# Delta-rule attention with two MoE layers: fewer warm-up products, shorter norms, and the first word fetch behind the solve's matrices

## The chip, the cores and the metric

One core of a Trainium2 chip runs the whole program in one launch. The metric is device time in microseconds. The kernel before takes 926.25 us (median of 3 runs, 925.52 to 926.77).

## The reference

Attention by the delta rule: for each of 4 x 8 heads a 48 x 48 state is updated over 768 steps, with normalised keys; then two MoE layers over all 3072 tokens.

```python
k_n = k / (np.linalg.norm(k, axis=-1, keepdims=True) + 1e-06)
for t in range(S):
    kt, vt, bt = (k_n[:, :, t], v[:, :, t], beta[:, :, t, None])
    y[:, :, t] = np.einsum('bhd,bhde->bhe', q[:, :, t], state)
    v_old = np.einsum('bhde,bhd->bhe', state, kt)
    state = state + bt[:, :, :, None] * np.einsum('bhd,bhe->bhde', kt, vt - v_old)
# x: attention output, 3072 x 384
h = np.maximum(x @ w_in, 0.0)                                # 384 x 2048
x = h * h @ w_out                                            # 2048 x 384
h = np.maximum(np.maximum(x @ w1, x @ w2), x @ w3)           # 384 x 768 each
return h @ w_out2                                            # 768 x 384
```

## The kernel before

The 768 steps are cut into 12 chunks of 64. Within a chunk the recurrence becomes a triangular system for each head. Its matrix is the Gram matrix of the chunk's keys, scaled by beta and by the squared norms. Each 64 x 64 system is solved as two halves of 32, one matrix on each of 128 partitions for two chunks at a time: that is the tile `M`, a view of `buf`, and `solve` on VectorE. The halves are merged with products on TensorE (`pZ`, `pW`), then come `pU` (the solved values), `pY` (the outputs), `pT` (a transpose) and `pD` (the state). After chunk 0 the MoE of chunk c runs on TensorE while the attention of chunk c + 1 is woven in between. The second MoE layer runs when all chunks are done.

All weights arrive as the 64-bit words of the arrays, two 32-bit halves to a value. ScalarE brings sign and exponent into place (`signed`: a Prelu at L103 and a Copy at L108), VectorE joins the halves (L120), ScalarE casts to the high part (L124), VectorE subtracts to get the low part (L128). A block of `w_in` is 384 KB; 12 blocks have tiles of their own (`rawp`), the others take turns (`raw`, `big`, `buf`). In this text "words" are these fetches, and a block's "signing" is L103 and L108.

The head, up to the first MoE product, runs in this order:

- Warm-up: NWARM products on TensorE (L716) on a zeroed tile, while the keys of chunks 0 and 1 are loaded (L772): first the keys of four half chunks, then their queries, alternately on the queues of SyncE (SP) and ScalarE.
- Gram products (`grams`, L784), four with keys alone, four with the queries. The first four are copied to SBUF by ScalarE and VectorE (L789) and stored to HBM as `kk` (L185). The second four are masked on VectorE (L798); two of them are stored by POOL (L800).
- `start32` (L292) loads beta (L299) and M: two DMAs per chunk, L302, from `kk` in HBM. Here chunk 0 is loaded by POOL, chunk 1 by SP.
- `prep` copies the diagonal (L247), then `norms` and `weighted` (L217 to L231) compute the norm `nm`, the row scale `r` = -beta/nm^2 and `a` = beta/nm^2. POOL clears the upper part of M with an affine select (L236), VectorE scales M by `r` (L237) and sets the diagonal (L238).
- `solve`: 30 pairs of a product and a sum (L283, L285) and a last scaling (L286).
- The result goes to HBM as `xt`, half by SP and half by ScalarE (L323), and `load_x` brings it back in another layout (`xb`, L342, `x1`, L350), half on each of the two queues for chunk 0.
- Meanwhile SP issues the words (L93) and the keys of chunks 2 and 3 (L833). ScalarE signs the first 12 blocks and copies the Gram matrices of chunks 2 and 3 (L841), POOL masks them (L846, eight operations).

Each engine carries out its instructions in one fixed order. For the greater part a scheduler sets that order when the program is built, from an estimate of its own of every instruction's time. `behind(a, b)` puts a after b on an engine without a wait. A DMA is issued by its engine in that order too and waits there for what it needs; it then runs beside the engine. DMAs from SP and ScalarE take one of eight semaphores in turn, and each waits until the earlier DMA with the same semaphore has landed.

Of the kernel before, what the change touches and what calls it, by code (L numbers as in the profile page):

```python
# [13 lines left out]
ALU = mybir.AluOpType  # L14
# [13 lines left out]
NF = FF // 128  # L28
# [11 lines left out]
def delta_moe(ctx, tc, kc, ab, kt, vt, beta, beta32, beta16, kq, w_in, w_out, w1, w2, w3, w_out2, out):  # L40
    nc = tc.nc
    vec, act, pool = nc.vector, nc.scalar, nc.gpsimd
# [31 lines left out]
    after, abs_after, cast_after, raw_after, x_after, raws = [], [], [], [], [], []  # L74
    parted, last_gl, last_gh = [], [None], [None]
    loose, casts = set(), []
    NR, NP = 4, 12
# [11 lines left out]
    def fetch(src, shape, dma):  # L89
        raw = raw_tile(shape)  # L90
        names = "k n" if len(shape) == 2 else "n"
        flat = "k (n t)" if len(shape) == 2 else "(n t)"
        raws.append(dma.dma_start(raw.rearrange(f"p {names} t -> p {flat}"), src).ins)  # L93
        for i in raw_after + x_loaded[-1:] * (NF < len(raws) <= 2 * NF):
            behind(raws[-1], i)
        return raw

# [52 lines left out]
    kcts, kss = [], []  # L150
# [32 lines left out]
    def kk_store(c, p, kk, dma=nc.sync):  # L183
        for t in range(2):
            dma.dma_start(kk_d[c][:, t, U2 * p:U2 * p + U2], kk[64 * t:64 * t + 64])  # L185
# [25 lines left out]
    def norms(ss, n, u, pool_):  # L211

        s0 = pool_.tile([128, n], F32, name="s0", tag="s0", bufs=1)
        r = pool_.tile([128, n], F32, name="r", tag="r", bufs=1)
        nm = pool_.tile([128, n], F32, name="nm", tag="nm", bufs=1)
        s0, r, nm = s0[0:u], r[0:u], nm[0:u]
        act.activation(out=s0, in_=ss, func=AF.Sqrt)  # L217
        vec.tensor_scalar(out=s0, in0=s0, scalar1=1e-19, scalar2=None, op0=ALU.max)
        vec.reciprocal(r, s0)
        vec.tensor_mul(out=r, in0=r, in1=ss)  # L220
        vec.tensor_add(out=r, in0=r, in1=s0)
        vec.tensor_scalar(out=nm, in0=r, scalar1=0.5, scalar2=1e-6, op0=ALU.mult, op1=ALU.add)
        return nm, r, s0

    def weighted(ss, n, u, bt, a, pool_):

        nm, r, s0 = norms(ss, n, u, pool_)
        vec.reciprocal(r, nm)
        vec.tensor_mul(out=s0, in0=r, in1=r)
        vec.tensor_mul(out=a, in0=s0, in1=bt)  # L230
        vec.tensor_scalar(out=r, in0=a, scalar1=-1.0, scalar2=None, op0=ALU.mult)  # L231
        return nm, r

    def strict(M, n, u, r, eng):

        selected[0] = pool.affine_select(out=M, in_=M, pattern=[[-1, n], [1, n]], compare_op=ALU.is_ge, fill=0.0, base=0, channel_multiplier=0).ins  # L236
        eng.tensor_mul(out=M, in0=M, in1=r.unsqueeze(1).broadcast_to([u, n, n]))  # L237
        eng.memset(diagonal(M, n), 1.0)  # L238

    selected, loaded, prep_after = [None], [None], []  # L240

    def diagonal(M, n):
        return M.rearrange("p j i -> p (j i)")[:, 0:n * n:n + 1]

    def prep(M, n, u, bt, a, pool_, eng=vec):
        ss = pool_.tile([128, n], F32, name="ss", tag="ss", bufs=1)[0:u]
        i = vec.tensor_copy(ss, diagonal(M, n))  # L247
        for j in prep_after:
            behind(i.ins, j)
        nm, r = weighted(ss, n, u, bt, a, pool_)  # L250
        strict(M, n, u, r, eng)
        return nm

    pinned, seen = {}, [None]
# [14 lines left out]
    def behind(ins, before):  # L269

        tc.add_manual_dep(ins, before.name, mybir.DependencyInfo(mybir.DependencyClass.NoSync, mybir.DependencyReason.DATA), reason="order")
# [108 lines left out]
    ops, normed, solved, solve_after, x_loaded = [], [], [], [], []  # L380
# [324 lines left out]
    if True:  # L705
        pro = ExitStack()
        pkp = pro.enter_context(tc.tile_pool(name="pkp", bufs=1))

        NWARM = 8
        ks_more = pkp.tile([128, 2, U2, C], F32, name="ks_more", tag="ks_more")  # L710
        warm = ks_more[:, 0, 0:2].rearrange("p u s -> p (u s)")
        vec.memset(warm, 0.0)
# [12 lines left out]
        def solve32(g, load=(nc.sync, nc.sync), store=((nc.sync,) * 2,) * 2, landing=0):  # L725
            M, a, ready, norm = start32(g, load)
            for _ in range(landing):
                yield
            if landing:
                prep_after[:] = last_gl  # L730
            nm = ready()
            if not g:
                normed.append(norm(nm))
            yield
            for n, i in enumerate(solve(vec, M, 32, 64 * len(HALVED[g]), a, tmp32)):
                for j in solve_after:
                    behind(i.ins, j)
                ops.append(i.ins)
                if g and n == (24 if g == 1 else 8):
                    norm(nm)  # L740
                yield
            finish32(g, M, store)
# [44 lines left out]
        for n, (c, p) in enumerate(todo):  # L787
            pg = grams(n, 0, (p1, at)[n % 2])
            kk_ends[p] = (vec.tensor_copy if p else act.copy)(kss[n][:, 0], pg).ins  # L789
            kk_store(c, p, kss[n][:, 0], (nc.sync, act)[p])  # L790
        p_stores = []
        for n, (c, p) in enumerate(todo):
            pg = grams(n, 1, (p1, at)[n % 2])
# [4 lines left out]
            prep_after[:] = [vec.tensor_mul(out=ks, in0=pg, in1=mask.unsqueeze(1).broadcast_to([128, U2, C])).ins]  # L798
            if c:
                p_stores.append(pool.dma_start(p_d[c][:, U2 * p:U2 * p + U2], ks).ins)  # L800
        first_solve = solve32(0, (pool, nc.sync), ((nc.sync, act), None))
        next(first_solve)
        prep_after.clear()
        raw_after[:] = loaded
# [241 lines left out]
```

## Time and profile before

| what | us |
|---|---|
| median of 3 runs | 926.25 |
| the profiled execution | 926.38 |
| its span, first to last instruction | 924.4 |
| TensorE busy, share of the span | 868.5, 94% |
| VectorE (DVE) busy | 475.8, 51% |
| ScalarE (ACT) busy | 376.0, 41% |
| GpSimd (POOL) busy | 146.6, 16% |

The rows come from the profiled execution; times are from the start of its span. A busy TensorE is not one at its peak: its matmuls are pipelined and their ends are modelled. The granted clock (PEclk) is a share of full speed, 1.00 or 0.50 at a moment, a mean in a stretch. A DMA's time to landing is counted from its issue. The DMA share is the mean busy share of 16 engines and can be above 1 where the packets of several queues overlap.

### The profile page before, as it was taken

The numbers are of one execution on the slowest core, as the hardware profiler recorded it, in microseconds if no ns is written. First come the engines' busy times: TensorE is split into PE (matmuls) and PEld (weight loads), VectorE is DVE, ScalarE is ACT, GpSimd is POOL, SyncE is SP. The second block draws the span as 40 slices with busy tenths as digits, with TensorE's granted clock in tenths as the row PEclk, the third lists the DMA queues.
The fourth block names the chain that finished last, engine by engine and source line by source line (L and its number), as shares of the span: only waits on it lengthen the run. The fifth ranks groups of instructions, "written<-read, shape, count | busy, mean of one in ns | idle before, by whom it ended". The sixth has DMA issues, their size and how long they took to land.

```text
span 924.4 us, 26481 instructions
## 1 busy us (share of the span) xinstructions
PE 868.5 (94%) x11422; PEld 843.0 (91%) x11422; DVE 475.8 (51%) x1068; ACT 376.0 (41%) x799; POOL 146.6 (16%) x241
## 2 busy tenths in 40 slices
PE   5439899899999999999999999999999999999998
PEld 5328888799999999999999999999999999999998
DVE  2978886288348734873586364457232322323221
ACT  1447853353445344544453556564121221212111
POOL 2323121411331133122313300002000000000000
PEclk8557999899999999999999999999999999999999
DMA  9987634732852284337434551334110101000000
GB/s 196 309 256 226 202 83 133 194 96 67 207 160 66 85 215 133 78 87 190 104 82 104 143 146 53 102 107 136 38 37 31 35 18 43 10 26 9 18 18 35
DMA packets 122596, 98.82 MB, mean 107 GB/s; under 512 B 77440, under 2 KB 102832, under 8 KB 122480
## 3 DMA queue, kind: packets, MB, share of 16 engines
q1 hardware_dynamic: 101824, 58.42, 24.1%
q0 software_dynamic: 11584, 32.22, 12.2%
q10 hardware_dynamic: 9072, 6.49, 2.4%
q8 instruction: 90, 1.47, 0.7%
q14 instruction: 26, 0.21, 0.1%
HBM read 72.45 MB, written 24.64 MB: 105 GB/s over the span
## 4 chain that ended last, share of the span: by engine, by line
PE 84%; DVE 8%; DMA 3%; ACT 2%; issue 1%; ACTq 0%; SPq 0%; DVEq 0%
PE p L954 24%; PE px L592 21%; PE p L572 20%; PE po L971 8%; PE pY L514 2%; PE pU L464 2%; DVE buf L283 2%; DVE buf L285 2%; PE pk L180 1%; PE pW L420 1%; DMA kct<-in_kc_dram 1%; PE pZ L411 1%; PE pA L445 1%; DMA raw<-in_moe_w_out_dram 1%; DVE gl L581 1%
## 5 line engine op out<-in xcount | busy, mean ns | idle before, releaser
L954 PE MATMUL p<-x_h,w 128*128 128x384 f32 x864 | 220.1, 336 | 0.0
L592 PE MATMUL px<-wout,gh 128*128 128x384 f32 x768 | 200.6, 342 | 0.4 <-ACT gh L580 0.4
L572 PE MATMUL p<-xh,win_h 128*128 128x256 f32 x576 | 169.6, 294 | 2.0 <-DVE gl L581 1.4
L572 PE MATMUL p<-xl,win_h 128*128 128x256 f32 x576 | 164.0, 285 | 0.3 <-DVE xl L536 0.3
L572 PE MATMUL p<-xh,win_l 128*128 128x256 f32 x576 | 164.0, 285 | 0.0
L954 PEld LDWEIGHTS p<-x_h,w 128*128 128x128 f32 x864 | 156.2, 188 | 0.0
L954 PE MATMUL p<-x_l,w 128*128 128x384 f32 x432 | 145.2, 336 | 0.0
L581 DVE TENSOR_TENSOR gl<-p,gh 128x512 fp32r<-128x512 f32 x96 | 66.2, 690 | 144.8 <-ACT gh L580 144.5
L592 PEld LDWEIGHTS px<-wout,gh 128*128 128x128 f32 x768 | 135.6, 190 | 1.9 <-ACT gh L580 0.6
L592 PE MATMUL px<-wout,gl 128*128 128x384 f32 x384 | 129.6, 337 | 0.0
L578 ACT ACTIVATE p<-p 128x512 f32<-128x512 f32 x96 | 55.9, 582 | 176.0 <-PE p L572 176.0
L572 PEld LDWEIGHTS p<-xh,win_h 128*128 128x128 f32 x576 | 111.0, 193 | 5.3 <-DVE gl L581 1.9
L572 PEld LDWEIGHTS p<-xl,win_h 128*128 128x128 f32 x576 | 111.1, 193 | 0.6 <-DVE xl L536 0.5
L572 PEld LDWEIGHTS p<-xh,win_l 128*128 128x128 f32 x576 | 111.4, 193 | 0.0
L960 DVE TENSOR_TENSOR mx<-p,mx 128x384 f32<-128x384 f32 x48 | 26.7, 557 | 126.7 <-PE p L954 126.6
L954 PEld LDWEIGHTS p<-x_l,w 128*128 128x128 f32 x432 | 81.2, 188 | 0.0
L962 ACT CAST hh<-mx 128x384 fp32r<-128x384 f32 x48 | 24.6, 513 | 125.8 <-DVE mx L961 125.8
L592 PEld LDWEIGHTS px<-wout,gl 128*128 128x128 f32 x384 | 72.7, 189 | 0.0
L285 DVE TENSOR_TENSOR buf<-buf 128x30 f32<-128x30 f32 (+9 forms) x180 | 61.1, 339 | 6.1
L283 DVE TENSOR_TENSOR buf<-buf 128x30 f32<-128x30 f32 (+9 forms) x180 | 60.6, 337 | 5.0
L580 ACT CAST gh<-p 128x512 fp32r<-128x512 f32 x96 | 56.4, 587 | 2.6
L579 ACT ACTIVATE p<-p 128x512 f32<-128x512 f32 x96 | 55.9, 583 | 2.6
(166 smaller groups left out, 1290.7 us busy)
## 6 DMA issues: line engine op xcount, KB each, us to landing
kq<-in_kc_dram POOLq DMA_DIRECT2D x22, 448.0 KB, 5.3
raw<-in_moe_w_dram SPq DMA_DIRECT2D x18, 384.0 KB, 3.5
raw<-in_moe_w_out_dram SPq DMA_DIRECT2D x16, 384.0 KB, 4.4
p<-p POOLq DMA_DIRECT2D x22, 256.0 KB, 3.6
rawp<-in_moe_w_in_dram SPq DMA_DIRECT2D x12, 384.0 KB, 10.3
v<-in_vt_dram POOLq DMA_DIRECT2D x24, 192.0 KB, 3.0
ktp<-in_kt_dram POOLq DMA_DIRECT2D x24, 192.0 KB, 3.6
x<-xs SPq DMA_DIRECT2D x48, 96.0 KB, 3.2
```

The lines of the kernel that those rows point to most:

```text
L283: eng.tensor_tensor(out=tv, in0=M[:, 0:j, j].unsqueeze(2).broadcast_to([u, j, m]), in1=M[:, j, j + 1:n].unsqueeze(1).broadcast_to([u, j, m ...
L285: yield eng.tensor_tensor(out=M[:, 0:j, j + 1:n], in0=M[:, 0:j, j + 1:n], in1=tv, op=ALU.add)
L572: pe.matmul(p1[:, j], w[:, k, f], x[c][:, k], start=n == 0 and j == 0, stop=n == 8, skip_group_check=True)
L578: act.activation(out=p1, in_=p1, func=AF.Relu)
L579: act.activation(out=p1, in_=p1, func=AF.Square)
L580: last_gh[0] = act.copy(gh, p1).ins
L581: last_gl[0] = vec.tensor_sub(out=gl, in0=p1, in1=gh.bitcast(F32)).ins
L592: g = pe.matmul(px[:, h, 0:DM], x[:, j, hs], w, start=f == 0 and i == 0, stop=f == NF - 1 and i == 2, skip_group_check=True)
L954: pe.matmul(p, w[i][:, k, fs], x[:, k], start=n == 0, stop=n == 8)
L960: vec.tensor_max(out=t, in0=ps[1], in1=t)
L962: act.copy(hh[:, f], t2)
L971: pe.matmul(po[:, 0:DM], x[:, f, js], w[:, f], start=i == 0, stop=i == 17)
```

## The change

It has five parts. The warm-up has 4 products instead of 8. The norm drops its factor 0.5 until later: `nm` is first twice the norm, and `r` is formed with -4 to make up for it. After M is scaled, two operations bring `nm` to its value and make `a` from `r`. The first word fetch gets a memset of one column of its tile, on POOL, ordered behind the affine select; the fetch waits for the memset, and the next eleven are ordered behind the first. Of the Gram stores three pairs go to SP and one to ScalarE, instead of two and two. M and beta of chunk 0 are loaded by SP and of chunk 1 by ScalarE.

```diff
--- before.py
+++ after.py
@@ -90,8 +90,10 @@
         raw = raw_tile(shape)
         names = "k n" if len(shape) == 2 else "n"
         flat = "k (n t)" if len(shape) == 2 else "(n t)"
+        if not raws:
+            behind(pool.memset(raw[:, 0, 0, 0:1], 0).ins, selected[0])
         raws.append(dma.dma_start(raw.rearrange(f"p {names} t -> p {flat}"), src).ins)
-        for i in raw_after + x_loaded[-1:] * (NF < len(raws) <= 2 * NF):
+        for i in raws[:1] * (1 < len(raws) <= NP) + raw_after + x_loaded[-1:] * (NF < len(raws) <= 2 * NF):
             behind(raws[-1], i)
         return raw
 
@@ -218,24 +220,23 @@
         vec.tensor_scalar(out=s0, in0=s0, scalar1=1e-19, scalar2=None, op0=ALU.max)
         vec.reciprocal(r, s0)
         vec.tensor_mul(out=r, in0=r, in1=ss)
-        vec.tensor_add(out=r, in0=r, in1=s0)
-        vec.tensor_scalar(out=nm, in0=r, scalar1=0.5, scalar2=1e-6, op0=ALU.mult, op1=ALU.add)
+        vec.scalar_tensor_tensor(out=nm, in0=r, scalar=2e-6, in1=s0, op0=ALU.add, op1=ALU.add)
         return nm, r, s0
 
     def weighted(ss, n, u, bt, a, pool_):
 
         nm, r, s0 = norms(ss, n, u, pool_)
-        vec.reciprocal(r, nm)
-        vec.tensor_mul(out=s0, in0=r, in1=r)
-        vec.tensor_mul(out=a, in0=s0, in1=bt)
-        vec.tensor_scalar(out=r, in0=a, scalar1=-1.0, scalar2=None, op0=ALU.mult)
+        vec.tensor_mul(out=s0, in0=nm, in1=nm)
+        vec.reciprocal(a, s0)
+        vec.scalar_tensor_tensor(out=r, in0=bt, scalar=-4.0, in1=a, op0=ALU.mult, op1=ALU.mult)
         return nm, r
 
     def strict(M, n, u, r, eng):
 
         selected[0] = pool.affine_select(out=M, in_=M, pattern=[[-1, n], [1, n]], compare_op=ALU.is_ge, fill=0.0, base=0, channel_multiplier=0).ins
-        eng.tensor_mul(out=M, in0=M, in1=r.unsqueeze(1).broadcast_to([u, n, n]))
+        scaled = eng.tensor_mul(out=M, in0=M, in1=r.unsqueeze(1).broadcast_to([u, n, n])).ins
         eng.memset(diagonal(M, n), 1.0)
+        return scaled
 
     selected, loaded, prep_after = [None], [None], []
 
@@ -248,7 +249,9 @@
         for j in prep_after:
             behind(i.ins, j)
         nm, r = weighted(ss, n, u, bt, a, pool_)
-        strict(M, n, u, r, eng)
+        scaled = strict(M, n, u, r, eng)
+        for t, x, by in ((nm, nm, 0.5), (a, r, -1.0)):
+            behind(vec.tensor_scalar(out=t, in0=x, scalar1=by, scalar2=None, op0=ALU.mult).ins, scaled)
         return nm
 
     pinned, seen = {}, [None]
@@ -706,7 +709,7 @@
         pro = ExitStack()
         pkp = pro.enter_context(tc.tile_pool(name="pkp", bufs=1))
 
-        NWARM = 8
+        NWARM = 4
         ks_more = pkp.tile([128, 2, U2, C], F32, name="ks_more", tag="ks_more")
         warm = ks_more[:, 0, 0:2].rearrange("p u s -> p (u s)")
         vec.memset(warm, 0.0)
@@ -787,7 +790,7 @@
         for n, (c, p) in enumerate(todo):
             pg = grams(n, 0, (p1, at)[n % 2])
             kk_ends[p] = (vec.tensor_copy if p else act.copy)(kss[n][:, 0], pg).ins
-            kk_store(c, p, kss[n][:, 0], (nc.sync, act)[p])
+            kk_store(c, p, kss[n][:, 0], (nc.sync, act)[n == 3])
         p_stores = []
         for n, (c, p) in enumerate(todo):
             pg = grams(n, 1, (p1, at)[n % 2])
@@ -798,7 +801,7 @@
             prep_after[:] = [vec.tensor_mul(out=ks, in0=pg, in1=mask.unsqueeze(1).broadcast_to([128, U2, C])).ins]
             if c:
                 p_stores.append(pool.dma_start(p_d[c][:, U2 * p:U2 * p + U2], ks).ins)
-        first_solve = solve32(0, (pool, nc.sync), ((nc.sync, act), None))
+        first_solve = solve32(0, (nc.sync, act), ((nc.sync, act), None))
         next(first_solve)
         prep_after.clear()
         raw_after[:] = loaded
```

The scheduler was run anew for the changed program, and its order differs beyond the lines that were changed. On ScalarE, around the end of the first solve, before (signing of block 11, the store of the solve's result, casts, the loads of `xb` and `x1`):

```order
L103 ACTIVATE rawp11_637<-rawp11_637 128x384
L108 ACTIVATE rawp11_637<-rawp11_637 128x384
L323 DMA xt0_117<-buf_144 32x1024
L124 CAST win_h_141<-rawp0_437 128x3x128
L124 CAST win_h_141<-rawp1_441 128x3x128
L124 CAST win_h_141<-rawp2_445 128x3x128
L342 DMA xb_146<-xt0_117 32x16x32
L124 CAST win_h_141<-rawp3_453 128x3x128
L124 CAST win_h_141<-rawp4_495 128x3x128
L342 DMA xb_146<-xt0_117 32x16x32
L350 DMA x1_667<-xt0_117 32x8x32 x2
L412 ACTIVATE k21_666<-pZ_708 128x256
```

and in the changed program, from the same store to the same loads:

```order
L326 DMA xt0_117<-buf_144 32x1024
L126 CAST win_h_141<-rawp0_433 128x3x128
L126 CAST win_h_141<-rawp1_438 128x3x128
L844 COPY buf_144<-pk_580 128x512
L126 CAST win_h_141<-rawp2_442 128x3x128
L844 COPY big_143<-pq_581 128x512
...
L105 ACTIVATE rawp11_634<-rawp11_634 128x384
L110 ACTIVATE rawp11_634<-rawp11_634 128x384
L126 CAST win_h_141<-rawp3_450 128x3x128
L126 CAST win_h_141<-rawp4_492 128x3x128
L345 DMA xb_146<-xt0_117 32x16x32 x2
L353 DMA x1_664<-xt0_117 32x8x32 x2
```

Blocks 7 to 11 are signed behind the store instead of ahead of it. The last two copies of the Gram matrices of chunk 3 also stand behind it, and so do five casts in place of three ahead of the first load of `xb`.

On POOL, from the end of its memsets, before:

```order
L723 MEMSET ktp1_148 128x16
L302 DMA buf_144<-kk0_93 32x32x32 x2
L236 AFFINE_SELECT buf_144<-buf_144 128x1024
L800 DMA p1_106<-ksr0_176 128x512
L800 DMA p1_106<-ksr1_177 128x512
L366 DMA v_676<-in_vt_dram 128x384
```

and now:

```order
L726 MEMSET ktp1_148 128x16
L236 AFFINE_SELECT buf_144<-buf_144 128x1024
L803 DMA p1_106<-ksr0_172 128x512
L803 DMA p1_106<-ksr1_173 128x512
L94 MEMSET rawp0_433 128x1
L369 DMA v_673<-in_vt_dram 128x384
```

The two loads of M are gone from this queue. The memset for block 0's tile stands behind both stores of `p1`.

On VectorE, from the maximum in `norms` to the solve's first step, before:

```order
L218 TENSOR_SCALAR s0_352<-s0_352 128x32
L219 RECIPROCAL r_353<-s0_352 128x32
L220 TENSOR_TENSOR r_353<-r_353,ss_350 128x32
L221 TENSOR_TENSOR r_353<-r_353,s0_352 128x32
L222 TENSOR_SCALAR nm_354<-r_353 128x32
L228 RECIPROCAL r_353<-nm_354 128x32
L229 TENSOR_TENSOR s0_352<-r_353 128x32
L230 TENSOR_TENSOR a32_342<-s0_352,b32_343 128x32
L231 TENSOR_SCALAR r_353<-a32_342 128x32
L237 TENSOR_TENSOR buf_144<-buf_144,r_353 128x1024
L238 MEMSET buf_144 128x32
```

and now:

```order
L220 TENSOR_SCALAR s0_348<-s0_348 128x32
L221 RECIPROCAL r_349<-s0_348 128x32
L222 TENSOR_TENSOR r_349<-r_349,ss_346 128x32
L223 SCALAR_TENSOR_TENSOR nm_350<-r_349,s0_348 128x32
L229 TENSOR_TENSOR s0_348<-nm_350 128x32
L230 RECIPROCAL a32_338<-s0_348 128x32
L231 SCALAR_TENSOR_TENSOR r_349<-b32_339,a32_338 128x32
L237 TENSOR_TENSOR buf_144<-buf_144,r_349 128x1024
L254 TENSOR_SCALAR nm_350<-nm_350 128x32
L254 TENSOR_SCALAR a32_338<-r_349 128x32
L238 MEMSET buf_144 128x32
```

Eight small operations between the maximum and the scaling of `buf` (M) have become six, and two stand behind the scaling.

## Rows read from the trace of the kernel before

**Rows 1.** The page's 40 slices, 23 us each; TensorE and DMA, tenths busy.

```profile
PE   5439899899999999999999999999999999999998
DMA  9987634732852284337434551334110101000000
```

**Rows 2.** The chain of waits, 0 to 110 us: start, length, what.

```profile
12.42 2.97 DMA kk<-ksr
15.77 5.67 DMA buf<-kk
...
51.44 1.24 DVE buf L286
...
55.72 3.48 DMA xb<-xt
59.33 1.11 PE pZ L411 x64
...
60.90 1.12 PE pW L420 x64
```

**Rows 3.** Timeline of ScalarE, 40 to 56 us: start, length, operation, idle before.

```profile
40.11 0.55 ACT L103 ACTIVATE rawp<-rawp 128x384 f32<-128x384 f32 x1 [5.78 <-DMA rawp<-in_moe_w_in_dram]
...
51.47 0.53 ACT L108 ACTIVATE rawp<-rawp 128x384 int32<-128x384 uint16 x1
...
53.17 1.48 ACT L124 CAST win_h<-rawp 128x384 fp32r<-128x384 f32 x3 [1.16 <-DVE rawp L120]
...
55.62 0.40 ACTq L342 DMA_DIRECT2D xb<-xt  x1
```

**Rows 4.** Groups by line, 0 to 20 us: count, busy us, mean ns.

```profile
L784 PE MATMUL pg<-kct 48*64 48x64 f32 x128 | 4.4, 219 | 0.2 <-issue 0.2
...
L716 PE MATMUL pw<-ks_more 128*128 128x128 f32 x16 | 3.8, 431 | 2.8 <-ACT ks_more L713 2.8
```

**Rows 5.** DMA issues at 15.4 (M) and 55.7 us (xb): KB, us to landing.

```profile
buf<-kk POOLq DMA_DIRECT2D x1, 128.0 KB, 3.7
...
xb<-xt ACTq DMA_DIRECT2D x1, 64.0 KB, 3.1
```

**Rows 6.** Timeline of VectorE, the norms of the first solve.

```profile
21.56 0.19 DVE L247 COPY ss<-buf 128x32 f32<-128x32 f32 x1 [5.75 <-DMA buf<-kk]
...
23.77 0.19 DVE L221 TENSOR_TENSOR r<-r,s 128x32 f32<-128x32 f32 x1
24.00 0.19 DVE L222 TENSOR_SCALAR nm<-r 128x32 f32<-128x32 f32 x1
```

**Rows 7.** Timeline of SP and POOL, 14 to 25 us.

```profile
14.75 1.62 POOL L302 DMA_DIRECT2D buf<-kk  x2 [10.65 <-DMA kk<-big]
16.59 2.27 SPq L93 DMA_DIRECT2D rawp<-in_moe_w_in_dram  x3
21.82 1.27 POOL L236 TENSOR_SCALAR_AFFINE_SELECT buf<-buf 128x1024 f32<-128x1024 f32 x1 [5.45 <-DVE ss L247]
23.04 1.14 POOL L800 DMA_DIRECT2D p<-ksr  x2
```

**Rows 8.** Stretches: us, five engines' busy us, PEclk, DMA share, GB/s.

```profile
2.50:5.00 2.50, 2.18 (x10) 2.19 (x11) 0.00 (x0) 0.25 (x2) 1.48 (x6) 1.00 1.22 237
16.20:21.40 5.20, 0.00 (x0) 0.00 (x0) 0.00 (x0) 0.00 (x0) 0.17 (x1) 0.64 1.15 192
21.40:51.80 30.40, 9.94 (x257) 9.12 (x257) 27.43 (x73) 15.38 (x37) 12.00 (x19) 0.50 1.06 324
```

**Rows 9.** Timeline of VectorE, three steps of the solve.

```profile
41.93 0.38 DVE L283 TENSOR_TENSOR buf<-buf 128x210 f32<-128x210 f32 x1
...
42.34 0.70 DVE L285 TENSOR_TENSOR buf<-buf 128x210 f32<-128x210 f32 x1
...
48.56 0.67 DVE L285 TENSOR_TENSOR buf<-buf 128x130 f32<-128x130 f32 x1
```

**Rows 10.** Timeline of TensorE, the merge of chunk 1.

```profile
109.25 0.95 PE L411 MATMUL pZ<-xb,k 32*32 32x32 f32 x64 [3.06 <-DVE v L449]
```

## The prediction

> **What bounds the kernel now.** I read the forty slices first [rows 1]. The 16 DMA engines are full in the first two slices (46 us), where TensorE is at 5 and 4 tenths; from slice 4 on it is at 8 or 9 almost throughout. So the head (0 to 76 us, until the first MoE product) is where a transfer or a wait costs time. What follows is a chain of products; a delay of the head is passed on, unless a later stage has slack.
>
> Second, the chain of waits in the head [rows 2]: the last store of the Gram matrices (12.42 + 2.97 = 15.39), the load of the solve's matrices M, its last part landing at 15.77 + 5.67 = 21.44, then VectorE's solve, which ends with the step at 51.44, at 52.66. The result goes to HBM (xt) and comes back (xb). pZ starts at 59.33 and pW at 60.90. The words of w_in do not appear in the chain, but they run beside it: ScalarE signs them without a pause from 40.11, when block 3 lands, to 52.00, as VectorE ends the solve [rows 3]. So two chains end together at 52, and the change moves both: it favours M and holds back the words.
>
> I count from two marks: S, when the copy of M's diagonal starts (21.56 [rows 6]), and T, the solve's end (52.66). S to T is 31.1 us, T to pW is 8.24 us.
>
> **Start of the solve.** Three edits act on S. Four warm-up products less: eight take 3.8 us [rows 4], so TensorE is free 1.9 us earlier. But the keys still arrive in their order and ScalarE's last Gram store waits for an earlier store, so I credit only 0.2 us at the last Gram store, 15.2 instead of 15.39; the bounds are 0 and 1.9. The M loads go from the POOL and SP queues to SP and ScalarE; the last pair is issued when the last Gram store has landed, as now, the second about 0.6 us later, at 15.8. The words are no longer beside them. Now the M loads take between 3.7 us (the first, almost alone [rows 5]) and 5.67 (the last, with words). I take 3.7, the load that met the fewest words: landing at 19.5, S = 19.6, a gain of 2.0. Ends: a landing as quick as the Gram store's 2.97 with the whole 1.9 gives 4.4; one 1 us slower gives 1.0.
>
> **Norms.** Before M is scaled, 8 small operations follow the maximum now, 6 afterwards; a step is 0.23 us (23.77 to 24.00 [rows 6]), so two fewer are 0.45 earlier. Two operations with the halves that were taken out come back between the scaling and the solve's first step, 0.2 us each, 0.4. I take 0 for the sum, between -0.3 and +0.3. In the later solves they stand on VectorE beside a busy TensorE, and I take 0 too.
>
> **The words.** Before, the first fetch is issued at 16.59 [rows 7]. Now it waits for a memset on POOL behind the affine select and both p stores. From S = 19.6: 0.26 to the select, 1.27 for it, 1.14 for the two stores [rows 7], 0.1 for the memset, about 22.4. That is 5.8 later, but the engines lose less. From 16.2 to 21.4 they moved 192 GB/s x 5.2 us = 1.0 MB [rows 8], of which 0.52 MB were M; the other 0.47 MB are 1.5 us at the 324 GB/s of the stretch behind it. Afterwards the first bulk transfer is the p store, issued at 21.1 and flowing 1.4 later (as the M loads, issued from 14.75 [rows 7], flow from 16.2), at 22.5; before, full flow began at 21.4. So every later transfer lands about 1.1 + 1.5 = 2.6 late, with 0.5 and 5.8 as ends. Block 3 lands at about 42.7 instead of 40.1, and the engines run empty at 54.4 instead of 51.8.
>
> **ScalarE's order: the price.** The order on ScalarE is new. Before its half of the xt store stood all 12 signings; now 7. The other five, ten operations, stand with two copies and five casts between the xt store and its loads of xb, on which pZ waits. First it must reach the store: 14 operations from block 3 on at 0.455 us each (26 operations in 40.11 to 52.00 [rows 3]) are 6.4, so 49.1, in time for T. Then T itself: while POOL masks, a step of the solve takes 0.70 us where one of the same size takes 0.38 [rows 9]; eight steps are hit so, the first at 42.34, the last at 48.56, which costs 2.6. Two of POOL's eight maskings now follow copies behind the xt store, so a quarter, 0.65, goes; 0 and 2.6 are the ends. T = 19.6 + 31.1 - 0.65 = 50.05, 2.6 earlier.
>
> From T: 0.5 to the first cast (52.66 to 53.17 [rows 3]), then 17 operations of 0.455, 7.75: xb is issued at T + 8.25 and T + 8.75; now the second is issued at 55.62, T + 2.96 [rows 3]. It lands 3.1 later [rows 5], so pZ starts at T + 11.85, and pW 1.57 behind it, as now (59.33 to 60.90): T + 13.4, 5.2 later against T than now. Ends: 0.5 less if these loads meet fewer others, 1.0 more if the next words, which SP fetches at that time, slow them as the M loads were slowed. SP's half alone would not be early either: its xt store stands behind words that end at 54.4.
>
> **Sum.** T 2.6 earlier, T to pW 5.2 longer: pW at 63.5, 2.6 later. Behind pW the order is the same until about 95 us, so nothing is won back. Around 104 to 116 us it changes: pZ of chunk 1 waits 3.06 us for a subtraction [rows 10] that stands behind a step that waits for a word; now it stands ahead of that step. But this pZ also moves ahead of eight wout products and six win products, so TensorE meets the wait earlier and is held nearly as long. I take 0.2 gained, between -1 and +1. That is +2.4 on the profiled execution's 926.38 (span 924.4), 928.8; the median of the runs is 0.13 under the profiled one, so I say 928.6.
>
> **The rivals.**
> *A. The solve wins the race: faster.* With the Gram store 1.7 more early, M landing in 2.97 (0.7), POOL's masking wholly behind the solve (1.95) and ScalarE's loads 0.5 sooner, T is 45.7 and the time 928.6 - 4.85 = 923.75. It decides from T below 46.3. For it: the 3.7 is one row, and the M loads are alone. Against it: the masking waits for copies that stand ahead of the xt store on ScalarE, so where they are late, the store is late. Chance 0.10.
> *B. Gain and loss cancel: no difference.* S 1.0 earlier than I take and ScalarE's loads 0.5 sooner: 927.1. Nothing in the rows excludes either. Chance 0.20.
> *C. The words decide: slower still.* If all 5.8 us reach block 3 (45.9), ScalarE gets to its store at 45.9 + 6.4 = 52.3, 2.2 behind T: 930.8. For it: ScalarE waits 5.78 for block 3 already [rows 3]. Against it: the engines work without a pause in between, so an issue that moves by 5.8 need not land by as much. Chance 0.15.
> *D. The clock in the Gram products: slower still.* The granted clock is at its higher level when the first products run [rows 8]. Should four warm-ups leave it at the lower level (1.2 GHz), the first four Gram products, 1.1 us each (four take 4.4 [rows 4]), would take 8.8, starting 1.9 earlier: the last ends 2.5 later, and so do the Gram store, T and pW: 931.1. The Trainium skill (TensorE: Matmul & The Clock Gate, "Part 1: The HAM clock gate") has an idle array at the lower level until it has been busy for a while; by it the time would be 931.1. The trace of the start does not agree, that behind 16 us does. Chance 0.05.
>
> **How the numbers follow.** The forecast has 0.50: 928.6, with its own range 927 to 930.3. A difference under 0.2% (924.4 to 928.1) cannot be told from no change. Faster: A, 0.10. Same: B and the forecast's lower part (0.15), 0.35. Slower: the rest of the forecast (0.35), C and D, 0.55. The range, 925.2 to 931.1, takes in B, C and D and the nearer half of the way to A; it leaves out A's end and what lies above D.
>
> **What would show it.** Right: the diagonal's copy at 19 to 20; the solve's end near 50; ScalarE signing blocks 7 to 11 behind its xt store; its loads of xb issued about 8 us behind the solve's end; pZ near 62. Wrong: xb issued within 4 us of that end, which breaks the ScalarE step; a solve's end before 46.3 (A); ScalarE still at block 6 when the solve ends (C); a granted clock under 1.00 before 10 us (D); pW before 61 with a time above 928.1, or pW after 63 with a time below 926, which would say that the later stages have slack.

## The result, and the profile after

The changed kernel takes 932.62 us (median of 4 runs, 932.29 to 934.52) against 925.88 of the kernel before beside it (924.90 to 926.77): a ratio of 1.0069, with a 95% interval of 1.0041 to 1.0097. Compared again on another chip the ratio was 1.0083 (1.0050 to 1.0117). Slower was forecast, and it is slower, but by 6.7 us and not by 2.4, and 932.62 lies above the range. The profiled run took 932.67, its span is 930.8.

The forty slices, TensorE and DMA, now 23.3 us each: the second slice (23 to 47 us) has TensorE at 1 tenth where it was at 4 [rows 1].

```profile
PE   4138989899999999999999999999999999999998
DMA  7998733842862285238433551334110101000000
```

The chain of waits in the head of the changed kernel (start, length, what):

```profile
7.46 5.79 DMA kk<-buf
...
13.85 3.69 DMA kk<-ksr
...
17.98 3.14 DMA buf<-kk
...
25.13 13.35 DMA rawp<-in_moe_w_in_dram
38.50 10.47 DMA rawp<-in_moe_w_in_dram
...
49.02 4.37 DVE rawp L122 x5
53.38 6.79 DMA xt<-buf
...
60.62 3.25 DMA xb<-xt
...
63.99 1.32 PE pZ L414 x64
...
65.77 1.12 PE pW L423 x64
```

The solve has left the chain of [rows 2]; the words of w_in stand in it instead, 25.13 to 48.97. M lands in 3.1 us (5.67 before), but it is asked for at 17.61, because the last Gram store lands only at 17.54 (15.39 before). Behind the solve, xt takes 6.79 us to HBM; it took 2.02.

VectorE at the start and the end of the first solve, to set beside [rows 6]:

```profile
21.24 0.19 DVE L248 COPY ss<-buf 128x32 f32<-128x32 f32 x1 [5.63 <-DMA buf<-kk]
...
25.94 0.16 DVE L286 TENSOR_TENSOR buf<-buf 128x30 f32<-128x30 f32 x1
...
47.87 1.23 DVE L289 TENSOR_TENSOR buf<-buf,a 128x1024 f32<-128x1024 f32 x1
49.02 4.69 DVE L122 SCALAR_TENSOR_TENSOR rawp<-rawp 128x384 int32<-128x384 int32 x5
```

S is 21.24, 0.32 earlier. T is 49.10, 3.6 earlier: S to T is 27.86 where it was 31.1. Of these 3.2, the way from S to the solve's first step has 0.4 (4.70 instead of 5.11), the solve itself 2.8: POOL's masking now begins at 48.34, beside the last scaling, and no other step meets it. The next work on VectorE stands beside the masking instead: five joins of words take 4.69 us (2.43 before, without the masking).

POOL and SP at the end of the hold, to set beside [rows 7]:

```profile
21.50 1.27 POOL L236 TENSOR_SCALAR_AFFINE_SELECT buf<-buf 128x1024 f32<-128x1024 f32 x1 [18.49 <-DVE ss L248]
22.71 1.24 POOL L803 DMA_DIRECT2D p<-ksr  x2
23.94 0.12 POOL L94 MEMSET rawp<- 128x1 int32 x1
24.09 1.65 SPq L95 DMA_DIRECT2D rawp<-in_moe_w_in_dram  x3
```

and the stretches (five engines' busy us, PEclk, DMA share, GB/s) beside [rows 8]:

```profile
2.50:5.00 2.50, 2.18 (x12) 1.96 (x13) 0.00 (x0) 0.26 (x2) 0.51 (x3) 1.00 1.18 235
16.20:21.40 5.20, 0.00 (x0) 0.00 (x0) 0.16 (x1) 0.00 (x0) 0.00 (x0) 0.57 0.54 87
21.40:24.00 2.60, 0.00 (x0) 0.00 (x0) 2.13 (x7) 0.23 (x1) 2.50 (x5) 0.50 0.02 8
24.00:25.40 1.40, 0.00 (x0) 0.00 (x0) 1.26 (x3) 0.00 (x0) 1.40 (x4) 0.50 0.98 307
24.00:46.33 22.33, 4.18 (x129) 3.75 (x129) 20.34 (x61) 3.65 (x11) 4.28 (x9) 0.50 1.02 272
```

and of the kernel before, until its block 3:

```profile
21.40:40.11 18.71, 5.56 (x129) 5.06 (x129) 16.60 (x48) 3.69 (x11) 6.68 (x11) 0.50 1.06 303
```

Full flow begins at 24.0 instead of 21.4, 1.3 behind the issue of the p stores, and the engines stay full until about 58.5 instead of 51.8. Until block 3 they move 272 GB/s where they moved 303.

The 1.00 in the first row is not a measured clock: the trace's first record of the clock begins at 6.67 (7.38 before). The Gram products of the changed kernel show the level ahead of it:

```profile
4.83 1.97 PE L787 MATMUL pg<-buf 48*64 48x64 f32 x32
6.59 1.14 PE L787 MATMUL pg<-big 48*64 48x64 f32 x32
```

The first 32 matmuls start 53 ns apart, those behind 6.67 about 29 ns apart. So by this spacing TensorE starts at the lower level (1.2 GHz) and rises during the first Gram product, with four warm-up products as with eight.

ScalarE, beside [rows 3]:

```profile
46.33 0.55 ACT L105 ACTIVATE rawp<-rawp 128x384 f32<-128x384 f32 x1 [6.83 <-DMA rawp<-in_moe_w_in_dram]
...
52.30 0.32 ACTq L326 DMA_DIRECT2D xt<-buf  x1
...
59.38 0.96 ACT L126 CAST win_h<-rawp 128x384 fp32r<-128x384 f32 x2
60.19 0.95 ACTq L345 DMA_DIRECT2D xb<-xt  x2
```

Block 3 is signed at 46.33 (40.11 before), ScalarE stores its half of xt at 52.30, 3.2 behind T, and asks for xb at 60.19. SP asks for its xb at 60.19 too: xt has just landed (53.38 + 6.79). pZ is 4.66 late, pW 4.87. The first MoE product, at 78.72, is 2.61 late (76.11 before): 2.26 of pW's delay are won back. The most of it is in the products of pY, first the kernel before, then the changed one:

```profile
68.30 3.32 PE L514 MATMUL pY<-u,p 64*64 64x48 f32 x57 [1.70 <-issue]
```

```profile
72.62 1.60 PE L517 MATMUL pY<-u,p 64*64 64x48 f32 x49 [0.83 <-issue]
```

The wait ahead of them is 0.9 shorter, and they run while the granted clock is at its higher level (from 71.52 to 74.94); before, it stayed at the lower one there. Then the middle adds to the delay, TensorE here and VectorE's step that holds pW, beside [rows 10]:

```profile
108.80 1.09 PE L414 MATMUL pZ<-xb,k 32*32 32x32 f32 x64 [2.25 <-DVE v L452]
...
119.13 0.99 PE L423 MATMUL pW<-k,xT 32*32 32x32 f32 x64 [2.38 <-DVE r L231]
```

```profile
112.69 0.36 DVE L118 TENSOR_SCALAR raw<-raw 128x384 int32<-128x384 int32 x1 [3.94 <-DMA raw<-in_moe_w_out_dram]
```

That word of wout was there for VectorE at 108.38 before. At the MoE's next start (the product that waits 0.62 us for xh) the changed kernel is at 135.85, the kernel before at 129.82: 6.0 late. From there to the end both need 795 us.

The way from the first MoE product to this mark, and a stretch within it, first of the kernel before, then of the changed one:

```profile
76.11:129.82 53.71, 49.58 (x728) 46.78 (x727) 44.22 (x112) 41.42 (x93) 10.67 (x17) 0.91 0.61 179
119.40:122.60 3.20, 3.20 (x92) 2.90 (x88) 2.93 (x11) 2.49 (x8) 1.16 (x2) 1.00 0.33 92
```

```profile
78.72:135.85 57.13, 51.11 (x729) 48.29 (x727) 44.67 (x112) 41.45 (x93) 12.85 (x20) 0.88 0.63 182
119.40:122.60 3.20, 3.20 (x65) 3.14 (x54) 3.13 (x11) 2.93 (x7) 1.31 (x2) 0.50 0.12 31
```

The same products take 3.4 longer. TensorE's waits of more than 50 ns are 5.4 there, against 3.5: that is 1.9. The other 1.5 is in the products: TensorE is busy for 51.11 instead of 49.58. In both kernels the clock falls to its lower level (1.2 GHz) behind pZ's wait (before from 109.78 to 113.20, now from 109.07 to 112.48); in the changed kernel it falls once more behind pW's, from 119.31 to 122.72.

### The profile page after: what moved, and what is told of

It reads as the page before. It is cut to its first block, busy times and chain, and to the rows that moved or that the text cites. A ratio compares the mean times of both kernels' runs of the same rounds, so it can differ in the third digit from the quotient of the medians.

```text
span 930.8 us, 26468 instructions
## 1 busy us (share of the span) xinstructions
PE 864.3 (93%) x11414; PEld 838.4 (90%) x11414; DVE 476.2 (51%) x1068; ACT 376.0 (40%) x799; POOL 146.4 (16%) x239
## 4 chain that ended last, share of the span: by engine, by line
PE 83%; DMA 8%; DVE 5%; ACT 2%; issue 1%; POOL 0%; SPq 0%; ACTq 0%; DVEq 0%
PE p L957 24%; PE px L595 20%; PE p L575 20%; PE po L974 8%; DMA rawp<-in_moe_w_in_dram 3%; PE pY L517 2%; PE pU L467 2%; DMA raw<-in_moe_w_out_dram 1%; PE pk L182 1%; PE pA L448 1%; PE pW L423 1%; DVE gl L584 1%; PE pZ L414 1%; DMA xt<-buf 1%; PE pT L535 1%
## 5 line engine op out<-in xcount | busy, mean ns | idle before, releaser
L288 DVE TENSOR_TENSOR buf<-buf 128x30 f32<-128x30 f32 (+9 forms) x180 | 59.7, 332 | 6.1
L286 DVE TENSOR_TENSOR buf<-buf 128x30 f32<-128x30 f32 (+9 forms) x180 | 59.2, 329 | 4.8
```

The costliest lines, as they stand in the source:

```text
L286: eng.tensor_tensor(out=tv, in0=M[:, 0:j, j].unsqueeze(2).broadcast_to([u, j, m]), in1=M[:, j, j + 1:n].unsqueeze(1).broadcast_to([u, j, m ...
L288: yield eng.tensor_tensor(out=M[:, 0:j, j + 1:n], in0=M[:, 0:j, j + 1:n], in1=tv, op=ALU.add)
```

## Experiments

Times are compared with the kernel before on the same chip. Runs of one kernel lay further apart on these chips (before: 919 to 930), so the traces decide where something waits and the ratios what it costs. The marks of all traces, in us; "empty" is the first whole microsecond behind 105 in which the DMA engines are busy less than half:

```
                        ratio (95%)              S     block 3   T     pZ    MoE   empty  xh    span
before                  1                       21.56  40.11  52.66  59.33  76.11  109  129.82 924.4
changed                 1.0069 (1.0041-1.0097)  21.24  46.33  49.10  63.99  78.72  113  135.85 930.8
e10 changed again       1.0083 (1.0050-1.0117)  20.84  45.94  48.69  64.10  80.90  115  135.85 930.4
e1  no hold             1.0012 (0.9985-1.0039)  30.96  39.58  61.60  68.16  83.57  120  136.71 929.1
e14 no hold again       one run                 32.75  41.38  63.40  70.13  85.09  120  139.52 934.7
e2  hold only           1.0041 (1.0020-1.0063)  21.43  45.43  51.02  63.53  78.88  115  132.38 926.7
e3  xb ahead of signing 1.0056 (1.0035-1.0078)  20.32  44.82  48.56  62.56  79.69  113  131.91 925.2
e4  xt by POOL          1.0126 (1.0100-1.0152)  20.53  45.53  48.38  67.54  81.78  116  138.80 934.1
e5  step moved          1.0081 (1.0053-1.0108)  20.64  45.88  48.49  63.04  79.15  113  131.17 923.8
e12 step moved again    1.0068 (1.0042-1.0094)  20.72  45.96  48.57  63.17  79.73  114  133.55 928.3
e6  shorter hold        1.0032 (1.0012-1.0052)  20.27  43.04  49.80  61.43  76.78  112  131.72 924.4
e7  xt ahead of words   1.0073 (1.0045-1.0102)  21.06  46.80  48.91  56.98  73.89  113  132.01 925.4
e8  warm-up, norms      0.9980 (0.9961-0.9998)  21.29  38.44  51.91  58.25  74.52  109  126.97 920.9
e16 the same again      0.9974 (0.9954-0.9994)  21.67  38.00  52.15  58.72  75.08  110  128.26 918.8
e9  old queues          1.0074 (1.0046-1.0102)  21.07  46.60  48.91  64.07  80.09  114  137.42 931.9
e11 Gram store first    1.0084 (1.0051-1.0117)  19.99  45.73  47.84  63.13  79.13  113  136.98 931.0
e13 eight warm-ups      1.0070 (1.0036-1.0104)  22.66  47.50  50.52  65.29  82.38  118  137.95 933.7
e15 e11 without hold    0.9975 (0.9956-0.9994)  21.78  37.57  52.42  58.96  75.04  110  127.47 922.2
```

**Which edit.** e1 takes the hold out, e2 puts it alone into the kernel before:

```diff
-        if not raws:
-            behind(pool.memset(raw[:, 0, 0, 0:1], 0).ins, selected[0])
```

> The changed kernel without the hold (no memset on the first word tile, no order among the first fetches); the other three edits stay. Theory W (the words, 6.2 us late, are the price): the signing of block 3 starts at 40 to 41 again, the signing of all twelve blocks stands ahead of the xt store, pZ starts at 58 to 61, time 924.5 to 928. Rival Q (the new stores and loads are the price, because the last Gram store lands at 17.5 instead of 15.4): the solve ends at 54 or later, pZ at 61 or later, time 929 or more.

> The kernel before with the hold alone (eight warm-up products, long norms, POOL and SQ queues for M as before). Theory W: M lands at 19 to 20 because no word flows, the solve ends at 47 to 48, but block 3 lands at 44 or later, pZ starts at 61 to 63 and the time is 928.5 to 931.5. Rival Q: the hold alone costs nothing, pZ at or before 59.3, time 924 to 926.5.

The hold alone costs 0.41%. Block 3 (45.43) comes as theory W said and pZ (63.53) 0.5 behind its range. M gains nothing by the hold: the diagonal is copied at 21.43, not at 19 to 20, and so T is 51.02, not 47 to 48. In e1 the price is gone from the median, and block 3 (39.58) and the time are as theory W said. pZ, at 68.16, is not, and the chain of waits of e1 shows why:

```profile
18.27 12.57 DMA buf<-kk
```

ScalarE's load of M, issued behind the first word fetches, takes 12.57 us and lands behind them; the solve starts 9.4 late. The twelve runs lie between 923.0 and 935.0. e14 is a second trace of this kernel, from a single run:

> A second trace of the kernel of e1. Theory R (a race between ScalarE's load of M, issued after the first word fetches, and these words): the landing differs from trace to trace; either behind the words again (the diagonal copied at 28 or later, time 928 or more) or ahead of them (copied at 21 to 24, time 922 to 926). Rival: the load always lands behind the words, and the time is 923 to 926 even so, because later stages have slack.

The load is late again, 14.91 us, and the run is the slowest of that kernel (936.60). Two traces of two with a late M, and a median of 924.91: I have no trace of a run near the median, so whether M is late there stays open.

e8 leaves warm-up and norms alone, e9 undoes the queues alone, e13 the warm-up alone (`NWARM = 8`):

```diff
-            kk_store(c, p, kss[n][:, 0], (nc.sync, act)[n == 3])
+            kk_store(c, p, kss[n][:, 0], (nc.sync, act)[p])
-        first_solve = solve32(0, (nc.sync, act), ((nc.sync, act), None))
+        first_solve = solve32(0, (pool, nc.sync), ((nc.sync, act), None))
```

> The kernel before with two of the four edits alone: four warm-up products and the shorter norms; no hold, M by POOL and SyncE as before. My steps for these two: 0 to 0.2 us each, so pZ at 58.5 to 59.5 and the time within 1.5 us of the kernel before. Rival: the earlier Gram products move the whole head by the warm-up's 1.9 us, pZ at 57 to 57.7, time 2 us less.

> The kernel of e8 once more, the fastest so far (ratio 0.998, upper end 0.9998), beside e15: 0.1 to 0.4% below the kernel before again, the diagonal copied at 21 to 21.6 and the wait of xh at 126.5 to 128.5.

> The changed kernel with the fourth edit undone: two pairs of Gram stores on SyncE and two on ScalarE, M and beta by POOL and SyncE as before; hold, warm-up and norms stay. If the edits add (hold +0.41%, warm-up and norms -0.20% against the kernel before), it is 0.1 to 0.4% slower than the kernel before, pZ at 61.5 to 63, and 3 to 4 us faster than the changed kernel in the same comparison: then the queues cost the rest. Rival: the queues cost nothing, and the time is that of the changed kernel within 1 us.

Warm-up and norms gain 0.20 and 0.26%, about 1.8 and 2.4 us, where I had 0.2 us for the one and nothing for the other. The queues cost nothing beside the hold: e9 is as slow as e10 of the same comparison. So all of the loss comes with the hold. It does not add up simply: the hold costs 0.41% alone, but beside warm-up and norms, which gain 0.20%, it brings the loss to 0.74%. Why stays open.

**Does ScalarE's order hold pZ?** e3 puts the signing of blocks 7 to 11 behind ScalarE's loads of xb and x1.

```diff
+        for s in late_signs:
+            behind(s, x_small[3])
```

> The changed kernel with the signing of blocks 7 to 11 put behind ScalarE's loads of xb and x1. Theory P (my step: 17 operations on ScalarE between the xt store and these loads set pZ): xb is issued on ScalarE by 57 and pZ starts at 59 to 61, time 927 to 929.5. Theory W (SyncE's xt store waits for a word transfer and lands behind the words): its xt store still lands at about 60, pZ stays at 63 to 64.5 and the time within 1 us of the changed kernel's, 931.5 to 933.5.

ScalarE of e3, and SP's store in its chain of waits:

```profile
53.83 0.99 ACT L126 CAST win_h<-rawp 128x384 fp32r<-128x384 f32 x2
59.04 0.95 ACTq L346 DMA_DIRECT2D xb<-xt  x2
```

```profile
52.27 6.74 DMA xt<-buf
```

ScalarE has nothing left to do ahead of xb from 54.8 on and still issues it at 59.04, when xt has landed. In the changed kernel the two end together, ScalarE's last cast at 60.33 and xt's landing at 60.17; here they are apart, and xb goes by xt. pZ starts at 62.56, not at the 59 to 61 of my step but 0.4 ahead of theory W's 63; the time, 930.27, is 1.2 below W's range.

**Why xt is late.** e4 gives xt, xb and x1 of chunk 0 to POOL (`((pool, pool), None)` and the queues of `load_x`); e7 leaves the queues and puts the fetches of blocks 8 to 11 and of four wout blocks behind the loads of xb:

```diff
+        for i in raws[8:NP + NR]:
+            behind(i, x_small[1])
```

> The changed kernel with the first solve's xt stores and their xb and x1 loads issued by POOL instead of SyncE and ScalarE. Theory W: free of the word transfers' order, the xt store is issued at 52 to 53 (behind POOL's masking), lands within 4 us, and pZ starts at 59.5 to 61.5; time 928 to 930.5. Rival E (the DMA engines are full of words, whichever queue asks): xt lands at 58 or later, pZ at 62 or later, time 931.5 or more.

> The changed kernel with the fetches of word blocks 8 to 11 and of the first four wout blocks put behind SyncE's loads of xb and x1, and the signing of blocks 8 to 11 behind ScalarE's. The hold stays, so block 3 is as late as in the changed kernel. Theory W (xt lands late because words lie ahead of it): xt lands at 52 to 55 instead of 60.2, pZ starts at 56 to 59, time 924 to 928. Rival E (the engines' delay returns later, because blocks 8 to 11 then come late for the first MoE products): pZ as early, but the first MoE product at 78.5 or later and the time 930 or more.

In e4 the first half of the store, issued at 53.45, lands at 58.90 (5.45 us), and POOL issues the loads from 59.18 on, the last of xb behind four of x1, so that pZ starts at 67.54. Rival E was right there: on another queue the store takes 5.45 us instead of 6.79 while the engines are full. How much of the rest is POOL's order e4 does not separate.

e7 also puts ScalarE's signing of blocks 8 to 11 behind its loads, which the lines above do not show. SP's timeline of e7 shows xt stored at T and back at once, and TensorE what comes of it:

```profile
48.93 0.33 SPq L326 DMA_DIRECT2D xt<-buf  x1
51.73 0.34 SPq L346 DMA_DIRECT2D xb<-xt  x1
```

```profile
80.04 0.53 ACT L126 CAST wout<-raw 128x384 fp32r<-128x384 f32 x1 [3.19 <-DMA kk<-ks_more]
...
85.46 1.01 PE L597 MATMUL px<-wout,gh 128*128 128x384 f32 x2 [5.27 <-ACT gh L585]
```

xt lands within 2.8 us, pZ starts at 56.98, 7 us earlier than in the changed kernel. The moved signing can have little part in that (e3, with the signing alone, moved pZ by 1.4): the rest is what the words ahead of xt cost pZ. The first MoE product comes at 73.89, not at the 78.5 or later of rival E. But the time does not follow. SP now issues its stores of the Gram matrices of chunks 2 and 3 behind the words; ScalarE waits 3.19 us for one of them, TensorE then 5.27 for its first gh, and xh is at 132.01.

**How long the hold is.** e6 ends it sooner, with a memset on VectorE right behind the copy of the diagonal:

```diff
-            behind(pool.memset(raw[:, 0, 0, 0:1], 0).ins, selected[0])
+            behind(vec.memset(raw[:, 0, 0, 0:1], 0).ins, copied[0])
```

> The changed kernel with a hold that ends sooner: the first word tile is marked by VectorE right behind the copy of M's diagonal, not by POOL behind the masking and the two p stores. Theory W: the first word fetch is issued at 21.3 to 22 instead of 24.1, block 3 is signed at 43 to 45 instead of 46.3, pZ starts at 60.5 to 62 instead of 64.0, time 926.5 to 930. Rival: the length of the hold does not matter, pZ at 63 or later, time 931 or more.

As theory W said: block 3 is signed at 43.04, pZ starts at 61.43, and the price falls to 0.32%; the first fetch goes out at 20.52, earlier than the 21.3 to 22 expected, since S is earlier too (20.27). The words' delay carries through, less hold, less loss.

**Why S gained so little.** e11 orders M's loads behind ScalarE's last Gram store. Before that, the store took one of the eight semaphores behind the first Gram store; now behind a load of beta.

```diff
+                if not g:
+                    behind(loaded[0], stored[0])
```

> The changed kernel with the loads of M ordered behind ScalarE's last Gram store, so that this store no longer follows the first Gram store on its completion counter but the small loads of beta. Theory L (that wait is why the solve's start gained 0.4 us and not 2): the store is issued at 10.8 to 11.8 instead of 13.3, the diagonal is copied at 19 to 20.2, the first word fetch goes out at 21.8 to 23, pZ starts 1 to 1.5 us earlier than in the changed kernel of the same comparison, time 1 to 2 us less. Rival: the store issued sooner shares the engines with the others and lands as late, the copy at 20.5 or later, no change of the time.

The chain of waits of e11:

```profile
12.59 2.91 DMA kk<-ksr
15.94 3.93 DMA buf<-kk
```

The store (issued at 12.07) lands at 15.50, M at 19.87, S is 19.99: the late end of the 19 to 20 that I had forecast, 1.2 us earlier than in the changed kernel. pZ is 1.0 earlier than in e10 (63.13 against 64.10), as expected, but xh 1.1 later (136.98 against 135.85), and the time does not move (1.0084 against 1.0083). So what the head gains is lost in the middle again.

e15 is e11 without the hold:

> Three of the four edits (warm-up, norms, M and beta by SyncE and ScalarE) without the hold, and with the loads of M ordered behind ScalarE's last Gram store as in e11. Theory R: ScalarE's load of M is issued at 15.3 to 16, ahead of the first word fetch or beside it, so the diagonal is copied at 20 to 22, no run is 4 us over the others, and the time is 0.1 to 0.4% below the kernel before. Rival: ScalarE's load still meets the words and is late in some runs, spread and median as in e1.

ScalarE asks for M at 15.33, beside the first fetch (15.08) and not behind it. M lands at 21.66, no earlier than in the kernel before:

```profile
21.78 0.19 DVE L247 COPY ss<-buf 128x32 f32<-128x32 f32 x1 [5.87 <-DMA buf<-kk]
```

0.9975 (0.9956 to 0.9994): faster than both kernels, as is e8/e16. It has warm-up and norms as they have, and is as fast as they are, so what M's place adds to them is not shown. Between e15 and e11 stands the hold alone: S 1.8 earlier with it, block 3 8.2 later, the time 0.9975 against 1.0084 (each against the kernel before on its own chip), about 1.1%.

**What the middle adds.** e5 and e12 move VectorE's step on the late wout word behind both subtractions of v and pA.

```diff
+            if len(shifts) == 16 and len(minus) > 1:
+                behind(g.ins, minus[1])
```

> The changed kernel with one step moved on VectorE in the middle: the shift of the wout word that waits for its transfer at 108.7 to 112.7 stands behind the second v minus pA of attention(1), not between the two. Theory O (that place holds attention(1), and with it pW, by the transfer's delay): the head is as in the changed kernel (pZ 63 to 64.5), pW of chunk 1 starts at 115 to 117 instead of 119.1, time 928.5 to 930.5. Rival D (the late transfer itself is the price, wherever the step stands): pW at 118 or later, time 931.5 to 933.5.

> The changed kernel once more, beside the others: pZ at 62.5 to 64.5, pW of chunk 1 at 117 to 120, 0.5 to 0.9% slower than the kernel before.

> The kernel of e5 once more, now beside the changed kernel: its trace agreed with theory O (pW of chunk 1 at 115.9) and its median with rival D. Theory O: pW at 117 or earlier again and a median 2 to 4 us below the changed kernel's. Rival D: the median within 1 us of the changed kernel's, and then the step's place sets the wait seen in a trace but not the time.

> The changed kernel with eight warm-up products instead of four. In the head this can only cost (up to 1.9 us at the Gram products), but with it the scheduler places the late wout step behind both v minus pA in the middle, as with the hold alone. Theory M (the order in the middle is the rest of the price beside the hold): the first MoE product is no earlier than in the changed kernel (78.7 to 80.9), the wait of xh at the end of attention(1) comes at 131.5 to 134 instead of 135.9, and the time is 2 to 4 us below the changed kernel's 0.83% over the kernel before, that is 0.3 to 0.6% over it. Rival H (the hold's delay is the whole price, the order none): 0.7 to 0.9% over the kernel before.

TensorE of e12, the merge of chunk 1 (PEld is its weight load):

```profile
109.96 0.82 PEld L418 LDWEIGHTS pZ<-xb,k 32*32 32x32 f32 x64 [2.86 <-DVE v L456]
...
118.27 0.74 PE L427 MATMUL pW<-k,xT 32*32 32x32 f32 x64 [0.31 <-DVE r L235]
```

VectorE of e12, a word of wout and the subtraction that pZ waits for:

```profile
105.11 0.36 DVE L119 TENSOR_SCALAR raw<-raw 128x384 int32<-128x384 int32 x1 [0.75 <-DMA raw<-in_moe_w_out_dram]
...
109.36 0.54 DVE L456 TENSOR_TENSOR v<-v,pA 128x384 f32<-128x384 f32 x1
```

TensorE of e13:

```profile
122.88 0.74 PE L423 MATMUL pW<-k,xT 32*32 32x32 f32 x64 [3.48 <-DVE r L222]
```

In e12 pW waits only 0.31, but pZ waits 2.86 for the subtraction, which ends at 109.90; VectorE has waited for an earlier word of wout ahead of it. pW starts at 118.27, not by 117, and the median is 1.5 us below e10's, with intervals that overlap: neither the 2 to 4 of theory O nor within 1 of it. e5 had pW at 115.9, as theory O said, and was as slow as the changed kernel by its ratio. e13 has that order too; its pW waits 3.48 for VectorE's r, and its ratio, 1.0070, is that of rival H. So the order of that step is at most a small part of the price. What these kernels share is the late stream of transfers. The stretches of the kernel before, and then of the changed one:

```profile
108.00:112.00 4.00, 2.75 (x72) 2.68 (x73) 3.62 (x10) 2.26 (x5) 0.00 (x0) 0.72 0.23 62
```

```profile
108.00:112.00 4.00, 3.20 (x71) 3.13 (x72) 0.75 (x2) 0.54 (x1) 0.00 (x0) 0.63 1.05 265
```

From 108 to 112 the engines are nearly idle before (share 0.23) and full afterwards (1.05), while VectorE waits. In the table, the four traces that run empty at 109 or 110 have xh at 127.0 to 129.8; with 112 or 113 it comes at 131.2 to 137.0, with 114 to 116 at 132.4 to 138.8, with 118 or 120 at 136.7 to 139.5. So the mark goes with xh but does not fix it: with 113 it differs by 5.8 (e5 and e11). TensorE's waits and clock differ there: from the first MoE product to xh e5 needs 52.02 us at a mean granted clock of 0.92, e11 57.85 at 0.90 with 7.2 of waits. What sets them apart I could not settle, and no run holds back the stream in the middle alone; that the late transfers are the price there is argued.

## Why the prediction was wrong

- **The words: the term that failed.** I had later transfers 2.6 late; block 3 was 6.2 late. The hold ends by a chain that hangs on S, and S was 21.24, not 19.6. So full flow began with the p stores, as read, but at 24.0, 2.6 behind the 21.4 of before, where I had 1.1. The 1.5 us for what had been moved earlier comes on top. That is 4.1; the other 2.1 are the rate, which I took as unchanged and which was 272 GB/s until block 3 instead of 303. Why it is lower stays open.
- **Start of the solve.** M did land in the shorter time (3.1, taken 3.7), but the last Gram store landed at 17.54 (taken 15.2). I had named its wait for an earlier store and not asked which: the first, stored at 7.46, took 5.79 us. e11 without that wait gives S = 19.99.
- **Norms.** Taken 0; S to the first step is 4.70 instead of 5.11, 0.41 gained. The two operations that come back start 0.1 us apart beside the others. The later solves, also taken as 0, no run shows by themselves.
- **T.** Taken 50.05, measured 49.10, for another reason: S was 1.6 later, but the masking went from all of the steps that it had slowed (2.8 us), not from a quarter of them (0.65).
- **ScalarE's order: the price.** The order was as read, and xb came far behind T (11.1 us, taken 8.25). But ScalarE was not the cause: e3 takes these operations away and pZ comes only 1.4 earlier. SP issued words of wout until 51.4, then its half of xt at 53.38, when block 9 had freed its semaphore; it landed behind the words at 60.17, 6.79 us for what took 2.02. I had that sentence, "behind words that end at 54.4", and gave the place no price. e7 gives it: with these words behind xt, and the signing moved, pZ is 7 us earlier.
- **The sum.** pW at 65.77, forecast 63.5. That "nothing is won back" behind it was wrong: 2.26 came back until the first MoE product, the most of it through the clock in the products of pY, which I had not priced.
- **The middle.** Taken as 0.2 gained; it lost 3.4 in this trace (first MoE product 2.6 late, xh 6.0 late). The step does stand behind the first subtraction, as read, but the wout word came 4.3 us later, and the second subtraction, and then pW, waited behind it. I had treated the order and not the transfers that it waits for. Of the 3.4, 1.9 are waits of TensorE and 1.5 slower products: the clock fell a second time, behind pW's wait, and the sum has no term for that.

Rival C came nearest by its mark: block 3 at 45.9 and ScalarE's store at 52.3 were met (46.33 and 52.30), and its 2.2 us over the forecast give pW at 65.7. I gave it 0.15 because "an issue that moves by 5.8 need not land by as much". In the end the issue moved by 7.5 (24.09) and block 3 by 6.2, so that objection held. And the agreement of pW is luck: C comes to it through ScalarE's order, for which pZ did not wait. C lacked the middle: 930.8 and not 932.7.

A fell: T was 49.10, not below 46.3. B fell: the ratio's interval, 1.0041 to 1.0097, leaves out no change. D fell, but my reading of [rows 8] was wrong: the 1.00 there is no record, and the products ahead of 6.67 run at the lower level. So the trace of the start does agree with the rule cited there. What saves the time is that the clock rises during the first Gram product with four warm-ups (6.67) as with eight (7.38), so the other three run at the higher level.

## What to carry to other kernels

Holding back a transfer stream that fills the DMA engines delayed here all of it (the first fetch by 7.5 us, block 3 by 6.2), and whatever was queued behind it. What the hold frees (here M, 5.67 to 3.1 us) is worth something only if that transfer, and not the stream, is what ends last. Before a hold is built, price the stream that it holds back: e15 has the other edits without it, lands M no earlier than the kernel before (S 21.78), and is about 1.1% faster than e11. And a delay that seems made up for at the next stage (pZ 4.7 late, first MoE product 2.6) can come back later, here in the 3.4 us that the middle added.

## What was not expected of the hardware

- A small load behind a filled queue: ScalarE's 128 KB of M took 12.57 (e1) and 14.91 us (e14) when issued 1.6 and 1.2 us behind the first words, on another queue than theirs, against 3.1 alone.
- VectorE beside POOL's masking: a step of the solve took 0.70 us with it and 0.38 without [rows 9]; when the masking had moved behind the solve, five joins of words took 4.69 us beside it instead of 2.43.
- TensorE's clock after a wait: the wait of 2.38 us for pW was followed by a stretch at the lower level (119.31 to 122.72), which the kernel before does not have there.
